# Linear attention and a gated feed-forward block in one planned stream: the last group's results in a room of their own, and the whole order planned anew

## The chip, the cores and the metric

One Trainium2 chip, one core of it. The metric is the device time of one execution in microseconds (us). A core has five engines that run beside each other, each in its own fixed order: TensorE (PE in the profile, its weight loads PEld), VectorE (DVE), ScalarE (ACT), GpSimd (POOL) and SyncE (SP). Any of SP, ACT and POOL can issue a DMA; the core's 16 DMA engines carry all of them out.

## What is computed

For 8 batches of 8 heads with 576 positions and 64 features per head, a linear attention with position weights, and on its output, as 4608 tokens of 512 features, a gated feed-forward block:

```python
r = np.maximum(x, 0.0)                                   # x is q or k
phi = np.concatenate([r * cos_w, r * sin_w], axis=-1)    # weights by position
kv  = np.einsum('bhsf,bhsd->bhfd', k_p, v)              # per head: (2*64) x 64
z   = np.sum(k_p, axis=2)
out = q_p @ kv / (q_p @ z + 1e-6)
...
g = x @ w_gate;  val = x @ w_val                         # 512 -> 1536
y = (g * sigmoid(g) * val) @ w_out                       # 1536 -> 512
```

(The last lines of each part are written shorter here.) Inputs and result are float32; inside, products take 16-bit operands and sum in float32.

## The kernel before

**Batches.** Each batch's q, k and v come by DMA on POOL into 16-bit tiles. ScalarE takes the relu of k, VectorE multiplies v by the two position weights, and 72 small matmuls (`kv_job`, L715) give kv and z. For batches from 2 on, the relu of q and its second, tangent-weighted half are written into the tile `r_q` (`feature_jobs`), which one DMA transposition on SP turns into `phit` (L838). Batches 0 and 1 go another way: TensorE turns their queries (`turned_tile`, L1296), one tile of 128 tokens in a burst of 8 transpositions, for tiles 4 to 8; a relu and a multiplication by tangents follow.

**Tiles.** A tile is 128 tokens (`tile_jobs`): 8 or more matmuls (L778, L784) into two banks of PSUM, ScalarE's denominator `den` (L796), VectorE's reciprocal `rec` (L802) and the multiplication into one of four slots `x` (L806). SP then turns x into `xT` by a DMA transposition (`turn_job`, L746); tiles 4 to 7 are turned by TensorE instead (L754). Two tiles at a time may hold their banks.

**Groups.** Four tiles make a group of 512 tokens; there are nine, 0 to 8. Gate and value products are done with seven block products instead of eight (`block_jobs`, L976; M1 to M7, with sums on VectorE and a ScalarE copy of M1 into the bank that M6 adds to), some value products plainly (`plain_val`, L1051). ScalarE takes silu (L1035), VectorE multiplies (L1060, L1071) into `ht`. The output product (`out_jobs`, L1141) is done with seven products P1 to P7 again; its four quarters are evicted into a room of the buffer `ob`: e11 (from P2), ev and then e22 (P7, P5), e21 (P4) and e12 (P3). VectorE's sums L1184 and L1198 join the products. A pair of tiles shares a room of 128 x 2 x 512 float32; there are two rooms. POOL stores groups 1 to 7 (L1110), SP group 0. In the last group P6, P5 and P3 are cut in halves, and `store_two_jobs` (L1236) stores each quarter as soon as it is written, on SP and ACT.

**The order.** Nothing in the loop order decides what runs when. Every operation is a `Job` with a duration per engine, the jobs it follows, the rooms it takes and gives back (banks, slots, `ob` rooms), and at build time `order_once` plans them all on the five engines: TensorE by rank, the others by due time, both shaken by a seed that changes every 10 us (`SEEDS`). A room is free again when the last job that gives it back is `done`, for a DMA some time after its planned end (`dma`, `tail`, `LATER`). Then each engine's instructions are emitted in the planned order, and the chip keeps that order; real waits are by semaphores. So what the plan puts ahead of an instruction on its engine runs ahead of it, whenever the chip is ready.

Of the kernel before, what the change touches and what calls it, by code (L numbers as in the profile page):

```python
# [11 lines left out]
FP32 = mybir.dt.float32  # L12
BF16 = mybir.dt.bfloat16
FP16 = mybir.dt.float16
AF = mybir.ActivationFunctionType
ALU = mybir.AluOpType
# [3 lines left out]
def kernel(  # L20
# [10 lines left out]
    nc = tc.nc  # L31
    B, H, S, D = q.shape
    P = 128
    G = H // 2
    J = G // 2
    SH = 64
    NC = S // SH
    d_model, d_ff = moe_w_gate.shape
# [14 lines left out]

    consts = ctx.enter_context(tc.tile_pool(name="consts", bufs=1))
    rawq = ctx.enter_context(tc.tile_pool(name="rawq", bufs=3))
    rel = ctx.enter_context(tc.tile_pool(name="rel", bufs=1))
    xtp = ctx.enter_context(tc.tile_pool(name="xtp", bufs=3))
    psum = ctx.enter_context(tc.tile_pool(name="psum", bufs=1, space=bass.MemoryType.PSUM))

# [27 lines left out]
    NSG, NM7, NX = 9, 3, 4  # L87
# [10 lines left out]
    late = phi_all.rearrange("p a b -> p (a b)")[:, LATE:LATE + 8 * J * D1 + 16 * J * SH]  # L98
    assert LATE >= NPHI and late.shape[1] + LATE <= 2 * NPHI
    ob_all = consts.tile([P, 2, 2, d_model], FP32, name="ob")  # L100
    raw_kv = consts.tile([P, 2, 2, G, NC, D], BF16, name="raw_kv")
    free_sg = list(range(NSG))
    raws = {}
# [62 lines left out]
    ident = consts.tile([P, P], BF16)  # L166
# [5 lines left out]
    late = late[:, 8 * J * D1:].rearrange("p (n e j c s) -> p n e j c s", n=4, e=2, j=J, c=2)  # L172
# [10 lines left out]
    def idle_products(n, cols=P):  # L183
# [34 lines left out]
        out=tab.rearrange("p c e d -> p (c e) d"),  # L218
        in_=csk.rearrange("p c e -> p (c e)").to_broadcast([P, NC * 2, D]),
# [5 lines left out]
    tanT = consts.tile([P, NC + 1, SH], FP16, name="tanT")  # L225
# [25 lines left out]
    for j in range(2):  # L251
        t = (phi_all.rearrange("p a b -> p (a b)")[:, 0:V2_1].rearrange(
            "p (g c e w) -> p g c e w", g=G, c=NC, e=2) if j else
            consts.tile([P, G, NC, 2, W], BF16, name=f"v2_{j}"))
# [21 lines left out]
    st = {}  # L276
# [234 lines left out]
    for word in words:  # L511
        word, _, eng = word.partition("@")
        op, a, b = re.match(r"([A-Za-z]+)(\d+)\.?(\d*)", word).groups()
        whole, a, part = b not in ("0", "1") or a != "0", int(a), int(b or 0)
# [39 lines left out]
        else:  # L554
            tiles = [int(x) for x in b]
# [25 lines left out]
    jobs = []  # L581
# [6 lines left out]
    def d2(n):  # L588
        return 70 + n / 1.92 + PAD
# [13 lines left out]
    def sc(n, sbuf=False):  # L603
        return 69 + n / 1.2 + (27 if sbuf else 0) + PAD

    def pe(occ, fn, key, **kw):
        return Job({"PE": occ}, fn, key=key, **kw)
# [7 lines left out]
    def bank(r):  # L615
        if r.n == 1:
            return banks[:, r.at[0]]
        lo, hi = sorted(r.at)
        return banks[:, lo:hi + 1:hi - lo]
# [15 lines left out]
    def relu_on(eng, out, in_):  # L635
        relu_op("act" if eng == "ACT" else "dve", out, in_)

    J_ = {("kv", 0): []}
    KV1_AT = 11.9
    TAN_AT = 9.0  # L640
    T8_AT = 15.5
    HALF_AT = (12.2, 12.6, 13.2, 13.8)
# [21 lines left out]
    tt = nc.vector.tensor_tensor  # L664
# [186 lines left out]
    def feature_jobs(b):  # L851

        loaded_q = [J_["load", b, "q"]] if b > 3 else []
        landed = 0.0 if loaded_q else LOADED["q", b]
        phis = []
        before = J_.get(("turned", b - 1), [])

        def home():
            if (b, "q") not in st:
                st[b, "q"] = rel.tile([P, G, NC, 2, D], BF16, name="r_q")  # L860
            return st[b, "q"]
        if b in PHI_ACT:
            for c in range(NC):
                for w in range(2):
                    def fn(j, c=c, w=w):
                        nc.scalar.activation(out=home()[:, :, c, w], in_=raws[b, "q"][:, :, c], func=AF.Relu,
                                             scale=tanq[:, c:c + 1] if w else 1.0)
                    phis.append(Job({"ACT": 412}, fn, after=loaded_q + before + J_["tanq"], rel=landed))
        else:
            for g in range(0, G, 2):  # L870
                def fn(j, g=g):
                    relu_on(j.eng, home()[:, g:g + 2, :, 0], raws[b, "q"][:, g:g + 2])
                phis.append(Job({"DVE": d4(1152)}, fn, after=loaded_q + before, rel=landed))
            for c in range(NC):
                def fn(j, c=c):
                    nc.scalar.activation(out=home()[:, :, c, 1], in_=raws[b, "q"][:, :, c], func=AF.Relu,  # L876
                                         scale=tanq[:, c:c + 1])
                phis.append(Job({"ACT": 430}, fn, after=loaded_q + before + J_["tanq"], rel=landed))
            J_["q_read", b] = list(phis)
        J_["phi", b] = phis  # L880
        return phis
# [232 lines left out]
    obs = {}  # L1114

    def ob_of(t):
        return ob_all[:, obs[t // 2].at[0], t % 2]

    def pair_of(p):
        return ob_all[:, obs[p].at[0]]  # L1120

    def out_jobs(tg, key):
        last = tg == NTG - 1
        t0 = tg * OUT
        ts = token_sum_jobs(tg)
        rooms = {0: Room("ob"), 1: Room("ob")}
        for p in range(2):
            obs[t0 // 2 + p] = rooms[p]

# [101 lines left out]
    def store_two_jobs(t, cols, after, queues):  # L1231
        for e in range(2):
            def fn(j, e=e):
                (b, c), (b1, _) = divmod(2 * t + e, NC), divmod(2 * t + 2 + e, NC)
                assert b == b1
                {"SP": nc.sync, "ACT": nc.scalar}[j.eng].dma_start(  # L1236
                    out=out_v[b, c:c + 3:2, :, cols].rearrange("c p f -> p c f"),
                    in_=pair_of(t // 2)[e * SH:(e + 1) * SH, :, cols])
            Job({queues[e]: 560}, fn, after=after, tail=3000.0)

    def plain_out_jobs(key):
        rooms = [Room("ob"), Room("ob")]
# [33 lines left out]
    for lo, hi in ((0, 2), (2, 4)):  # L1276
        def fn(j, lo=lo, hi=hi):
            o = raws[1, "k"][:, lo:hi]
            relu_on(j.eng, o, o)
# [2 lines left out]
    kv_job(1, (0, KV1_AT / 16), rk + vm)  # L1282
    plain_out_jobs((0, 0.76, 0.015))

    def turned_tile(t, key):

        r = Room("bank")
        slots = [(0, NC - 1), (1, 0)] if t == 4 else [(1, 2 * t - 9), (1, 2 * t - 8)]
        mine = late[:, 2 * (t % 2):2 * (t % 2) + 2]

        def fn(j):
            ps = bank(r).bitcast(BF16).rearrange("p (y e s) -> p y e s", e=2, s=SH)
            for jj in range(J):
                for n, (b, c) in enumerate(slots):
                    for i in range(2):
                        nc.tensor.transpose(out=ps[i * D:(i + 1) * D, 2 * jj + n].rearrange("p e s -> p (e s)"),  # L1296
                                            in_=raws[b, "q"][:, 2 * jj + i, c], identity=ident)
        mm = pe(240, fn, key, after=[], get=[r], rel=LOADED["sa" if t < 6 else "sb", 1])
        for b, c in slots:
            J_.setdefault(("q_read", b), []).append(mm)  # L1300
        old = J_["tile_mm"][-2:-1] if t > 5 else []

        def fn(j):
            relu_on(j.eng, mine[:, 0].rearrange("p e j c s -> p e (j c) s"),
                    bank(r).bitcast(BF16).rearrange("p (y e s) -> p e y s", e=2, s=SH)[:, :, 0:2 * J])
        re_ = Job({"ACT": sc(512), "DVE": 352}, fn, after=[mm] + old, put=[r])
        c0 = NC - 1 if t == 4 else 2 * t - 9

        def fn(j):
            tt(out=mine[:, 1].rearrange("p e j c s -> p (e j) (c s)"), in0=mine[:, 0].rearrange("p e j c s -> p (e j) (c s)"),  # L1310
               in1=tanT[:, c0:c0 + 2].rearrange("p c s -> p (c s)").unsqueeze(1).to_broadcast([P, 2 * J, P]), op=ALU.mult)
        J_["turned tile", t] = [re_, Job({"DVE": d2(512)}, fn, after=[re_])]

    J_["tile_mm"] = []
    for t in range(4, 9):
        turned_tile(t, (0, (HALF_AT[t - 4] - 0.6) / 16) if t < 8 else (0, T8_AT / 16))
        tile_jobs(t, (0, HALF_AT[t - 4] / 16) if t < 8 else (1, 1.0), t < 8)
        J_["tile_mm"].append(J_["tiles", 1][-1])
    J_["kvd_free"] = J_["tile_mm"][0:1]

    def fn_t(n):
# [71 lines left out]
    for tg in range(1, NTG):  # L1393
        b = tg + 2
# [40 lines left out]
    TILES_AT_ONCE = 2  # L1435
    DMA_MARGIN = 0.0
    EARLY = 9000.0
    SIZE = {"sg": NSG, "m7": NM7, "x": NX, "ob": 2, "tile": TILES_AT_ONCE}
    AHEAD = 18000.0
    SLACK = 1600.0  # L1440
    LOOSE = 8000.0
# [11 lines left out]
    def order_once(nominal, seeds):  # L1453
# [8 lines left out]
        while ready:  # L1462
            j = ready.pop()
# [79 lines left out]
        while n_left:  # L1543
# [43 lines left out]
            j.done = t + j.engs[e] + (TAIL[e] if j.tail is None else j.tail)  # L1587
            if j.dma:
                moved[0] = max(t + j.dma[0], moved[0]) + j.dma[1]
                j.done = moved[0] + LATER  # L1590
            at[e] = t + j.engs[e]
            n_left -= 1
            for r in j.get:
# [14 lines left out]
            for s, _ in succ[j]:  # L1608
                missing[s] -= 1
                if not missing[s]:  # L1610
                    learn(s)
        return max(j.done for j in jobs if "PE" in j.engs)

    RESERVE = 1
    LATER = 2200.0
    SEEDS = (9809, 17028, 79282, 23851, 85677, 79440, 78841, 69575, 80126, 93490, 42418, 59393, 0, 20917, 95217, 13415, 85644, 62013, 51029, 24021, 0, 84984, 14392, 87705, 77482, 88068, 0, 0)
    SHAKE = 1500.0
    WINDOW = 10000.0
    PACK = True
# [40 lines left out]
```

## Time and profile before

| | |
|---|---|
| median of three runs | 301.06 us (301.02 to 301.19) |
| the profiled execution | 300.46 us, span 298.7 us, granted TensorE clock 0.998 |
| busy TensorE, VectorE, ScalarE, POOL | 291.3, 250.9, 199.5, 70.6 us |
| transposition of a tile on SP (xT<-x, 28 times) | median 4.5 us from issue to landing |
| last group's stores (L1236, 8 times) | 2.4 to 3.0 us from issue to landing |

The span runs from the first instruction to the last; the profiled execution's own time is 1.8 us longer. The page lists busy time by engine, the chain of work that ended last (followed back from the last instruction through whatever released each step), and groups of instructions; queries of the trace list waits, timelines of a stretch, and one tile's or line's instructions. In a timeline line stand the start in us, the time, the engine, the line in the kernel, the operation and its tiles, and in brackets the idle time before it and what ended it. "ACTq" and "SPq" are DMA issues. A matmul's record is longer than its place in the stream: matmuls of 256 columns start every 109 ns.

### The profile page before, as it was taken

The numbers are of one execution on the slowest core, as the hardware profiler recorded it, in microseconds if no ns is written. First come the engines' busy times: TensorE is split into PE (matmuls) and PEld (weight loads), VectorE is DVE, ScalarE is ACT, GpSimd is POOL, SyncE is SP. The second block draws the span as 40 slices with busy tenths as digits, with TensorE's granted clock in tenths as the row PEclk, the third lists the DMA queues.
The fourth block names the chain that finished last, engine by engine and source line by source line (L and its number), as shares of the span: only waits on it lengthen the run. The fifth ranks groups of instructions, "written<-read, shape, count | busy, mean of one in ns | idle before, by whom it ended". The sixth has DMA issues, their size and how long they took to land.

```text
span 298.7 us, 8071 instructions
## 1 busy us (share of the span) xinstructions
PE 291.3 (98%) x3244; PEld 238.4 (80%) x3244; DVE 250.9 (84%) x513; ACT 199.5 (67%) x421; POOL 70.6 (24%) x126
## 2 busy tenths in 40 slices
PE   8999999999999999999999999999999999999992
PEld 4697465676777888888988888888888898888882
DVE  7878996978977898989979997988879868976972
ACT  6664346979558986797699588996475556645520
POOL 7954620030042130221233203200220050002020
PEclk9999999999999999999999999999999999999999
DMA  7999999999989999269899892770370074002025
GB/s 259 228 196 198 202 206 208 201 217 204 193 137 172 157 213 160 72 126 189 131 177 234 143 155 69 145 160 2 73 142 2 0 131 83 2 2 70 2 70 142
DMA packets 71781, 40.89 MB, mean 137 GB/s; under 512 B 48704, under 2 KB 68672, under 8 KB 71744
## 3 DMA queue, kind: packets, MB, share of 16 engines
q0 software_dynamic: 24992, 24.91, 49.8%
q1 hardware_dynamic: 46320, 15.08, 27.1%
q8 instruction: 25, 0.41, 0.6%
q10 hardware_dynamic: 432, 0.39, 0.4%
q14 instruction: 12, 0.10, 0.1%
HBM read 37.75 MB, written 9.44 MB: 158 GB/s over the span
## 4 chain that ended last, share of the span: by engine, by line
PE 88%; DVE 5%; DMA 4%; ACT 1%; issue 1%; ACTq 0%; DVEq 0%
PE banks L976 43%; PE banks L1141 23%; PE banks L1250 4%; PE banks L437 4%; PE banks L903 4%; DMA xT<-x 3%; PE banks L715 2%; PE banks L784 2%; PE banks L1051 2%; DMA wo_sb<-in_v_dram 1%; DVE ht L1060 1%; DVE sums L1092 1%; DVE v L292 1%; PE banks L778 1%; PE banks L371 1%; ACT sg L1035 1%
## 5 line engine op out<-in xcount | busy, mean ns | idle before, releaser
L1110 POOL DMA_DIRECT2D out_dram<-ob x56 | 29.4, 533 | 148.6 <-ACT ob L629 104.7
L1035 ACT ACTIVATE sg<-banks 128x512 bf16<-128x512 f32 x72 | 41.3, 596 | 9.9 <-PE banks L976 9.5
L627 ACT COPY banks<-banks 128x512 f32<-128x512 f32 (+1 forms) x53 | 30.2, 577 | 17.8 <-PE banks L1141 6.0
L1071 DVE TENSOR_TENSOR ht<-sg,banks 128x512 f16<-128x512 bf16 x60 | 40.3, 680 | 1.7 <-PE banks L976 1.6
L976 PEld LDWEIGHTS <-wg_sb 128*128 128x128 f16 x384 | 36.9, 98 | 5.5 <-issue 0.4
L1141 PEld LDWEIGHTS <-ht 128*128 128x128 f16 x384 | 37.0, 98 | 4.9 <-issue 0.3
L976 PEld LDWEIGHTS <-wgs_sb 128*128 128x128 f16 x368 | 35.6, 98 | 5.5
L996 DVE TENSOR_TENSOR banks<-m,banks 128x512 f32<-128x512 f32 x44 | 30.3, 691 | 7.0 <-ACT m L627 4.3
L629 ACT ACTIVATE ob<-banks 128x512 f32<-128x512 f32 x34 | 19.9, 595 | 22.7 <-PE banks L1141 22.3
L976 PEld LDWEIGHTS <-wv_sb 128*128 128x128 f16 x320 | 31.2, 98 | 3.9 <-DVE x L806 0.2
L976 PE MATMUL banks<-kvt,wgs_sb 128*128 128x256 f16 x236 | 33.6, 273 | 0.0
L1141 PEld LDWEIGHTS <-sums 128*128 128x128 f16 x288 | 27.9, 98 | 3.6 <-DVE sums L1092 0.2
L627 ACT COPY m<-banks 128x512 f32<-128x512 f32 x44 | 25.6, 589 | 6.5 <-PE banks L976 6.4
L976 PE MATMUL banks<-xT,wg_sb 128*128 128x256 f16 x192 | 28.5, 273 | 0.3 <-ACT banks L627 0.3
L1141 PE MATMUL banks<-wo_sb,ht 128*128 128x256 f16 x192 | 25.9, 273 | 0.0
L1141 PE MATMUL banks<-wt_sb,sums 128*128 128x256 f16 x192 | 24.3, 273 | 0.0
L976 PE MATMUL banks<-xT,wv_sb 128*128 128x256 f16 x160 | 23.9, 273 | 0.0
L806 DVE TENSOR_TENSOR x<-banks,rec 128x512 f16<-128x512 f32 x32 | 21.7, 687 | 2.0 <-DMA xT<-x 0.3
L976 PE MATMUL banks<-kvt,wg_sb 128*128 128x256 f16 x168 | 23.1, 273 | 0.0
L1141 PE MATMUL banks<-wt_sb,ht 128*128 128x256 f16 x192 | 22.8, 273 | 0.2 <-DVE banks L1184 0.2
L876 ACT ACTIVATE r_q<-raw_q,tanq 128x256 bf16<-128x256 bf16 x45 | 20.1, 503 | 0.0
L1035 ACT ACTIVATE sg<-m 128x512 bf16<-128x512 f32 x24 | 15.1, 629 | 7.1 <-DVE m L1004 7.0
(157 smaller groups left out, 542.4 us busy)
## 6 DMA issues: line engine op xcount, KB each, us to landing
out_dram<-ob POOLq DMA_DIRECT2D x56, 128.0 KB, 3.4
raw_kv<-in_k_dram POOLq DMA_DIRECT2D x7, 576.0 KB, 6.9
raw_q<-in_q_dram POOLq DMA_DIRECT2D x12, 288.0 KB, 9.6
raw_kv<-in_v_dram POOLq DMA_DIRECT2D x6, 576.0 KB, 8.9
out_dram<-ob SPq DMA_DIRECT2D x13, 128.0 KB, 2.5
wg_sb<-in_moe_w_gate_dram POOLq DMA_DIRECT2D x5, 256.0 KB, 8.8
wv_sb<-in_moe_w_val_dram POOLq DMA_DIRECT2D x5, 256.0 KB, 9.4
wo_sb<-in_v_dram SPq DMA_DIRECT2D x2, 576.0 KB, 4.1
```

The costliest lines, as they stand in the source:

```text
L437: nc.tensor.matmul(out=st["f", tg, fc, lo][i], lhsT=(wg_sb, wv_sb)[i][:, kc, fs], rhs=xT[tg][:, ts, kc], start=(kc == 0), stop=(kc == KC - 1))
L627: nc.scalar.copy(out=out, in_=in_)
L629: nc.scalar.mul(out=out, in_=in_, mul=mul)
L806: tt(out=one(x_all, x).rearrange("p (y e d) -> p e y d", e=2, d=D), in0=view()[:, :, :, 0:D], in1=rec_all[:, t % 4].rearrange("p (e y) o - ...
L876: nc.scalar.activation(out=home()[:, :, c, 1], in_=raws[b, "q"][:, :, c], func=AF.Relu, scale=tanq[:, c:c + 1])
L903: nc.tensor.matmul(out=bank(r), lhsT=w[:, kc, fc * P:(fc + 1) * P], rhs=xT[tg][:, :, kc], start=(kc == 0), stop=(kc == KC - 1))
L976: nc.tensor.matmul(out=to[:, i], lhsT=a[:, c, 2 * u + i], rhs=x()[:, :, c], start=first and i == 0 and c == 0, stop=c == KH - 1, skip_grou ...
L996: tt(out=bank(c), in0=one(m7_all, m).rearrange("p i x -> p (i x)"), in1=bank(b), op=ALU.add)
L1035: nc.scalar.activation(out=gates(rooms[w])[:, :, jh * HT:(jh + 1) * HT], in_=src, func=AF.Silu, scale=DOWN)
L1071: tt(out=ht[:, 4 * u + w:4 * u + w + 3:2, jh * HT:(jh + 1) * HT], in0=gates(rooms[w])[:, :, jh * HT:(jh + 1) * HT], in1=src.rearrange("p ( ...
L1110: {"POOL": nc.gpsimd, "SP": nc.sync, "ACT": nc.scalar}[j.eng].dma_start(out=out_v[idx // NC, idx % NC][:, cols], in_=ob_of(t)[e * SH:(e + ...
L1141: nc.tensor.matmul(out=to, lhsT=a[:, kc, i * P:(i + 1) * P], rhs=b[:, kc], start=first and kc == 0 and i == 0, stop=kc == HC - 1, skip_gro ...
```

## The change

Three things. The last group's two rooms are no longer those of `ob`: they lie in the memory of `r_q`, which becomes a constant tile (kind "last ob" in the plan). The queries of tiles 4 and 5, and of 6 and 7, are turned in one burst of 16 transpositions into one bank; tile 8 stays alone. And the plan is made anew: the last group's stores have other durations in it, the plan's end is that of the last job of all and not of the last TensorE job, and the seeds are others. So the order of nearly every engine past the first 32 us differs, with the same work. Line numbers behind the head grow by one.

```diff
-    rel = ctx.enter_context(tc.tile_pool(name="rel", bufs=1))
...
+    rq_all = consts.tile([P, G * NC * 2 * D], BF16, name="r_q")
+    ob_last = rq_all[:, 0:8 * d_model].bitcast(FP32).rearrange("p (a b f) -> p a b f", a=2, b=2)
...
-                st[b, "q"] = rel.tile([P, G, NC, 2, D], BF16, name="r_q")
+                st[b, "q"] = rq_all.rearrange("p (g c w d) -> p g c w d", g=G, c=NC, w=2)
...
-        return ob_all[:, obs[p].at[0]]
+        return (ob_last if obs[p].kind == "last ob" else ob_all)[:, obs[p].at[0]]
...
-        rooms = {0: Room("ob"), 1: Room("ob")}
+        rooms = {n: Room("last ob" if last else "ob") for n in range(2)}
...
-            Job({queues[e]: 560}, fn, after=after, tail=3000.0)
+            Job({queues[e]: 660}, fn, after=after, tail=1300.0, dma=(700.0, 560.0))
...
-    def turned_tile(t, key):
+    def turned_tiles(ts, key):
...
+            for m, t in enumerate(ts):
+                for jj in range(J):
+                    for n, (b, c) in enumerate(slots[t]):
+                        for i in range(2):
+                            nc.tensor.transpose(out=turned(m)[i * D:(i + 1) * D, 2 * jj + n].rearrange("p e s -> p (e s)"),
+                                                in_=raws[b, "q"][:, 2 * jj + i, c], identity=ident)
+        mm = pe(200 + 236 * len(ts), fn, key, after=[], get=[r], rel=LOADED["sa" if ts[-1] < 6 else "sb", 1])
...
-    for t in range(4, 9):
-        turned_tile(t, (0, (HALF_AT[t - 4] - 0.6) / 16) if t < 8 else (0, T8_AT / 16))
-        tile_jobs(t, (0, HALF_AT[t - 4] / 16) if t < 8 else (1, 1.0), t < 8)
-        J_["tile_mm"].append(J_["tiles", 1][-1])
+    for ts in ((4, 5), (6, 7), (8,)):
+        turned_tiles(ts, (0, (HALF_AT[ts[0] - 4] - 0.6) / 16) if ts[0] < 8 else (0, T8_AT / 16))
+        for t in ts:
+            tile_jobs(t, (0, HALF_AT[t - 4] / 16) if t < 8 else (1, 1.0), t < 8)
+            J_["tile_mm"].append(J_["tiles", 1][-1])
...
-    SIZE = {"sg": NSG, "m7": NM7, "x": NX, "ob": 2, "tile": TILES_AT_ONCE}
+    SIZE = {"sg": NSG, "m7": NM7, "x": NX, "ob": 2, "last ob": 2, "tile": TILES_AT_ONCE}
...
-                j.done = moved[0] + LATER
+                j.done = moved[0] + (j.tail if j.tail < LATER else LATER)
...
-        return max(j.done for j in jobs if "PE" in j.engs)
+        return max(j.done for j in jobs)
...
-    SEEDS = (9809, 17028, 79282, 23851, 85677, ...)
+    SEEDS = (0, 62553, 49105, 61770, 0, ...)
```

## The prediction

> **What bounds the kernel now.** I read the page first, then the chain of work that ended last, then the waits of TensorE, and then the timelines of the stretches that these pointed to.
>
> ```profile
> PE 291.3 (98%) x3244; PEld 238.4 (80%) x3244; DVE 250.9 (84%) x513; ACT 199.5 (67%) x421; POOL 70.6 (24%) x126
> ...
> PE 88%; DVE 5%; DMA 4%; ACT 1%; issue 1%; ACTq 0%; DVEq 0%
> ```
>
> TensorE bounds it: it is busy nearly everywhere and carries 88% of the chain. The granted clock is 0.998, so nothing is to be had there. Only three things can move the time: TensorE's own work, the places where it waits, and the end behind its last matmul. The waits of TensorE and of its weight loads (us in total, times, longest) are few:
>
> ```profile
> PE banks L976 <- ACT banks L627: 0.3, 1, 0.3
> PE banks L1141 <- DVE banks L1184: 0.2, 1, 0.2
> ...
> PEld L784 <- DVE x L806: 0.6, 2, 0.3
> PEld L1051 <- DVE x L806: 0.6, 1, 0.6
> ```
>
> A busy matmul covers part of a wait, so I measured each by the starts of consecutive matmuls against their usual distance (109 ns for 256 columns, 216 ns for 512). Past 32 us that gives 0.24 at 73.5 (L1051), 0.34 at 82 (L1141), 0.43 at 87 (L976), 0.20 at 128.3 and 0.20 at 129.2 (L784), 0.12 at 217 and 0.05 at 187: 1.6 us in all. The end, from the chain, and ScalarE's timeline there:
>
> ```profile
> 284.63 8.09 PE banks L1141 x74
> 292.75 0.43 DVE ob L633
> 293.18 0.35 ACTq L1236
> ...
> 293.74 0.60 ACT ob L629
> ```
>
> ```profile
> 292.81 0.72 ACTq L1236 DMA_DIRECT2D out_dram<-ob  x1
> 293.74 0.60 ACT L629 ACTIVATE ob<-banks 128x512 f32<-128x512 f32 x1 [5.41 <-PE banks L1141]
> 293.90 1.66 ACTq L1236 DMA_DIRECT2D out_dram<-ob  x2
> ```
>
> The copy at 293.74 is e11, the quarter whose product P2 was complete four microseconds earlier. It stands behind a store issue in ScalarE's order, since its room was group 7's. The last SP and ACT stores, issued at 294.54 and 294.93, are e11's, and the span ends at 298.7.
>
> **The end: last group's own room.** It adds no instruction. In the new emitted order ScalarE's copies ev and e11 both stand before its first store issue and wait for TensorE alone; e11's stores go out first, on SP and on ACT. What is late next is e12: the last matmul ends at 293.37, the VectorE copy of its second half runs 293.40 to 293.83, and its two stores can be issued at 293.86 (SP) and about 293.9 (ACT). So the last issue comes 1.0 us earlier (294.93 - 293.9). Issue to landing at L1236 is 2.4 to 3.0 us, median 2.8, before and after; the last landing then moves by 0.9 to 1.05 with ACT's own rows (2.8 to 3.0), by up to 1.5 with the shortest. I take **-1.0**. The VectorE waits for group 7's stores that vanish took about 0.05 us each beside the 0.69 us copy of e21, so they are worth nothing. The own room reuses r_q, whose last reader (the transposition of batch 7, 7.5 us from its issue at 193.0) is long done; cost nothing.
> In the new tail P6a, P6b and P5a follow each other without P2b between. P5a needs VectorE's sum of P6a: 0.31 us from a last matmul's start to a VectorE start (293.09 to 293.40), 0.43 for the sum, 0.06 back, 0.80, against 7 x 0.109 = 0.76: **+0.05**.
> The Trainium skill ("DMA: Bandwidth & Descriptors", "Anatomy of one DMA") gives a DMA some 2.0 us fixed plus its bytes over 436 GB/s. For 128 KB that would be an estimate of 2.3 us and a last landing 0.5 us sooner than mine. The rows 2.4 to 3.0 disagree upwards, and they decide.
>
> **Turned queries.** Forty transposes before, forty after. Tiles 4 and 5 already stood together; tiles 6 and 7 did not. The chain has x16 at 0.57 us and x8 at 0.34, so joining one pair saves 2 x 0.34 - 0.57 = **0.1**. Both relus then read one bank; tile 7's first use is two microseconds off in either order, so nothing waits.
>
> **The order anew**, counted from the emitted orders. TensorE's instructions are the same 3244. Visits to the 16-bit batch-side products (L715, L778, L784, L1296) between the others cost about 0.09 us at their entry; there are 36 before and 34 after: **-0.2**.
> Waits that go. At 87, M6 followed M1 after 0.87 us of other matmuls, while the ScalarE copy between them takes 0.58 plus two handovers and stood behind another; now a whole kv product (1.2 us) stands between: -0.43. At 128 and 129 four tiles stood within 3 us, with two tile rooms; now the third comes 2.6 us or more behind the first, and tile to x takes 2.0 to 2.3: -0.4. Together **-0.85**.
> A wait that grows. VectorE idles for tile 10's x in this stretch, and SP shows why:
>
> ```profile
> 72.13 0.64 DVE L1060 TENSOR_TENSOR ht<-sg,banks 128x512 f16<-128x512 bf16 x1
> 73.03 0.69 DVE L806 TENSOR_TENSOR x<-banks,rec 128x512 f16<-128x512 f32 x1 [0.26 <-DMA xT<-x]
> ```
>
> ```profile
> 53.45 7.57 SPq L838 DMA_TRANSPOSE phit<-r_q  x1
> 61.13 3.08 SPq L1110 DMA_DIRECT2D out_dram<-ob  x5
> 64.31 1.28 SPq L746 DMA_TRANSPOSE xT<-x  x1
> 65.63 0.62 SPq L1110 DMA_DIRECT2D out_dram<-ob  x1
> ```
>
> Tile 10 takes the x slot of tile 8, whose transposition (8.6 us, in the chain 64.31 to 72.90) must have read it. In the new order all eight group-0 stores stand between batch 2's transposition and tile 8's; before, two went ahead and one behind, so three more now, at 3.08 / 5 and a gap, 0.64 us each. Against that, the two stores that no longer precede it leave 256 KB less traffic beside the slow 7.57 us transposition (others of its kind issue in 4.6), so I put its end 1.0 sooner. Tile 8's issue: 60.0 + 0.1 + 8 x 0.64 = 65.2; between 64.3 (all 1.9 regained) and 66.5 (nothing, and features 0.3 later). Plus 8.6: landing 73.8, bounds 72.9 and 75.1. Without that wait x could start at 73.4, for tile 11's reciprocal, whose input ScalarE ends at 73.05, now stands ahead of it. So x starts at about 73.9 and TensorE's tenth value product (L1051), which takes x's bank, at 73.9 + 0.69 + 0.06 = 74.65; TensorE gets there at 73.64 (73.54 now, with 0.1 us more matmuls ahead of it in the new order): 1.0 instead of 0.24. From x to the sum L1184 VectorE has 8.4 us of work (before 8.5), and P5 behind it waits 0.2 instead of 0.34. Sum 1.2 against 0.58: **+0.65**, bounds 0 and 1.8. Nothing gives this back: VectorE is full until 88, TensorE afterwards.
> The Trainium skill ("DMA: Bandwidth & Descriptors", "Issuing engines are not separate DMA queues") says that transfers of all issuers run on the same 16 engines and interleave. This speaks against the new order: eight stores and 1.7 MB of loads (k, v and q) share them with this one transposition. The trace agrees, 8.6 us against a median of 4.5 for its kind. By that rule alone, with no traffic taken away, the upper bound above would hold.
> Other new waits: every stage is ordered anew; five waits of 0.05 to 0.43 came with the old order outside this stretch, 1.0 in all, so between 0 and 1.0; I take **+0.3**, since the new order has fewer tiles close together. One eviction-side job moves from VectorE to ScalarE (a 0.4 us relu): nothing.
>
> **Sum:** -1.0 + 0.05 - 0.1 - 0.2 - 0.85 + 0.65 + 0.3 = -1.15. The profiled execution took 300.46 (span 298.7 and 1.8 around it); so 299.3 there. The median of the three runs is 301.06, 0.6 higher, so **299.9**.
>
> **Rivals.**
> A, the gain is eaten at 73 us: tile 8's transposition lands at 75.1 or so, TensorE waits 2.3 + 0.2 there, +1.9 instead of +0.65. Then 301.1, no change that can be seen (0.2%, 0.6 us, is about what a measurement tells). For it: the 8.6 us row and the three stores. Against: less traffic before it.
> B, slower: the loads of batch 3 and batch 4's queries, which wait only for batch 2's transposition, go out earlier, and the transposition of tile 8 ends only with them, at about 76.5 as they ended before. x then starts at 76.6, TensorE loses 3.9 there, +3.3: 302.6. It decides when that landing passes 75.6, where the loss reaches 2.4 and the whole +0.6. Against: before, its packets moved beside the loads, at a quarter of the engines' time.
> C, the own room does nothing: SP, with five store issues, ends as late as before. Then -0.15, 300.9. Against: SP's e12 issue at 293.86 follows its previous one, ending at 293.41, with room to spare.
> The Trainium skill ("DMA: Bandwidth & Descriptors", "Queues, rings and completion order") has each engine take turns between queues, packet by packet. By that rule B would have no chance; the rows of one such transposition do not exclude it.
>
> **Chances.** Forecast 0.62 (its own range 299.0 to 300.4), A 0.23, C 0.05, B 0.10. Faster 0.62, same 0.28 (A and C), slower 0.10. The range, 298.9 to 301.4, takes in A and C and leaves out B and some low tail.
>
> **What would show it.** Right: e11's copy before ScalarE's first store issue, and about 4.3 us from the last matmul's end (293.37) to the span's end (298.67) instead of 5.3; no wait at 87 and 128; VectorE's x of tile 10 at 73.9, behind its DMA. Wrong: x of tile 10 past 75, or a wait of TensorE of over 0.5 us anywhere behind 90, or the span's end still 5 us behind the last matmul.

## The result and the profile after

The changed kernel takes 305.55 us in the median of four runs (304.43 to 306.71); the kernel before took 301.04 beside it. The ratio is 1.0152, with a 95% interval of 1.0105 to 1.0199: **slower by 4.5 us**, where 1.2 us faster was forecast and 301.4 was the upper end of the range. The profiled execution took 306.71 us with a span of 304.9, against 300.46 and 298.7. A second series of the same kernel gave 306.1 (run e5 below).

The page of the changed kernel, busy time and then the chain of work that ended last:

```profile
PE 294.3 (97%) x3244; PEld 239.2 (78%) x3244; DVE 250.8 (82%) x512; ACT 199.3 (65%) x422; POOL 70.0 (23%) x126
...
PE 36%; DMA 3%; DVE 2%; issue 0%; ACT 0%; DVEq 0%
```

The work is the same, yet TensorE is busy 3.0 us longer with the same 3244 matmuls (1.0 of it in the head, the first 32 us, which the change leaves alone), and the rest of the span's growth is idle time. The chain covers only 41% of the span: it goes back to a load at 176.53 and breaks off there, so it does not show where most of the time was lost. The waits of TensorE do (us in total, times, longest):

```profile
PE banks L1052 <- DVE x L807: 2.9, 1, 2.9
PE banks L977 <- DMA xT<-x: 1.2, 1, 1.2
PE banks L187 <- DVE zeros L182: 1.0, 1, 1.0
PE banks L785 <- DVE x L807: 0.9, 3, 0.3
```

The third of these stands in the head. Of the waits of before, those at 87 (L976 behind a ScalarE copy) and at 128 and 129 are gone, as forecast. In their place stands one of 2.9 us at the plain value product that waits for VectorE's x. VectorE's timeline there, and SP's:

```profile
73.10 0.44 DVE L803 RECIPROCAL rec<-den 128x8 f32<-128x8 f32 x2
76.42 1.29 DVE L807 TENSOR_TENSOR x<-banks,rec 128x512 f16<-128x512 f32 x2 [2.88 <-DMA xT<-x]
```

```profile
53.68 6.39 SPq L839 DMA_TRANSPOSE phit<-r_q  x1
60.12 5.33 SPq L1111 DMA_DIRECT2D out_dram<-ob  x8
65.55 14.71 SPq L747 DMA_TRANSPOSE xT<-x  x4
```

Tile 10's x starts at 76.42, not at 73.03 as before nor at 73.9 as forecast: it takes the slot of tile 8, whose transposition, issued at 65.55 behind all eight stores of group 0, landed at 76.3. TensorE, by the starts of its matmuls, stands still for 3.06 us from 74.1. Then comes a second loss. TensorE's timeline, and the same stretch in windows of 5 us (busy times and counts of PE, PEld, DVE, ACT and POOL, then the granted clock, the DMA share and GB/s; the last line is the kernel before):

```profile
73.25 1.03 PE L1052 MATMUL banks<-xT,wv_sb 128*128 128x512 f16 x4
77.17 4.45 PE L1052 MATMUL banks<-xT,wv_sb 128*128 128x512 f16 x12 [2.90 <-DVE x L807]
```

```profile
70.00:75.00 5.00, 4.27 (x40) 2.58 (x38) 3.50 (x9) 5.00 (x14) 0.00 (x0) 1.00 1.27 185
75.00:80.00 5.00, 2.83 (x8) 1.12 (x9) 3.08 (x5) 2.48 (x5) 0.00 (x0) 0.76 0.85 139
80.00:85.00 5.00, 4.99 (x42) 3.61 (x41) 4.37 (x9) 1.12 (x3) 0.00 (x0) 0.90 0.90 171
...
75.00:80.00 5.00, 5.00 (x41) 3.71 (x39) 5.00 (x10) 2.27 (x5) 0.00 (x0) 1.00 1.32 153
```

Twelve matmuls of 512 columns take from 77.17 to 81.46, 4.29 us instead of 12 x 0.216 = 2.59. Eight of them start 427 ns apart, twice the usual distance, and the granted clock of those windows is 0.76 and 0.90 where before it was 1.00: in the trace it stands at 0.50 for 3.4 us, from 77.6 to 81.0, and at 1.00 on both sides. That is 1.7 us more, and with the head's 1.0 it is most of what TensorE's busy time grew by.

**Where the 6.2 us of the profiled span went:** wait at 74: 3.06 instead of 0.24, +2.8; slow clock behind it, +1.7; waits behind 90: 1.27 at 173.6 (a transposition of a tile), 1.23 in three at 186 to 190 (x), 0.41 at 250.5 and 0.26 in small ones, 3.2 instead of 0.6, +2.6; waits at 82 and 87, -0.6; the end, -0.9; bursts and visits, some -0.2; and the head, code that the change leaves alone, +0.6 (TensorE's L693 at 32.77, L692 before at 32.18). Sum 6.0.

The end came as forecast. ScalarE's timeline there:

```profile
293.90 0.59 ACT L630 ACTIVATE r_q<-banks 128x512 f32<-128x512 f32 x1
295.15 0.60 ACT L630 ACTIVATE r_q<-banks 128x512 f32<-128x512 f32 x1 [0.66 <-PE banks L1142]
295.78 5.80 ACTq L1237 DMA_DIRECT2D out_dram<-r_q  x3
```

Both copies now stand ahead of the first store issue. From the last matmul's end (300.45) to the span's end (304.90) are 4.45 us, before 5.31.

### The profile page after: what moved, and what is told of

It reads as the page before. It is cut to its first block, busy times and chain, and to the rows that moved or that the text cites. A ratio compares the mean times of both kernels' runs of the same rounds, so it can differ in the third digit from the quotient of the medians.

```text
span 304.9 us, 8061 instructions
## 1 busy us (share of the span) xinstructions
PE 294.3 (97%) x3244; PEld 239.2 (78%) x3244; DVE 250.8 (82%) x512; ACT 199.3 (65%) x422; POOL 70.0 (23%) x126
## 5 line engine op out<-in xcount | busy, mean ns | idle before, releaser
L630 ACT ACTIVATE ob<-banks 128x512 f32<-128x512 f32 x32 | 18.9, 596 | 21.7 <-PE banks L1142 21.6
L293 DVE TENSOR_TENSOR v<-raw_kv,tab 128x1152 bf16<-128x1152 bf16 x27 | 19.5, 748 | 1.4 <-DMA raw_kv<-in_v_dram 1.4
```

Of the source, the lines that this page charges most:

```text
L293: nc.vector.tensor_tensor(out=v2s[b == 1][:, g, :, :, 0:D], in0=(first if b == 0 and g == 0 else {"v": raw_of(b, "v")})["v"][:, g].unsquee ...
L630: nc.scalar.mul(out=out, in_=in_, mul=mul)
```

## The experiments

**Theory:** tile 8's transposition came late because loads and stores hold up its queue; the late x idled TensorE, and the idle time lowered the clock. **Rivals:** the loss stands in the other waits of the new order; the transposition is slow wherever it is issued; the slow matmuls have a cause of their own; it takes the whole new order to make the loss. The table shows all runs, each beside the kernel before on the same chip. The wait is that of TensorE at 73 to 74, from the starts of its matmuls.

| run | median us | ratio to before (95%) | wait at 74 | slow matmuls |
|---|---|---|---|---|
| changed | 305.55 | 1.0152 (1.0105 to 1.0199) | 3.06 | yes |
| e1 room alone, old order | 300.4 | 0.9984 (0.9975 to 0.9993) | 0.49 | no |
| e2 changed, own slot for tile 10 | 299.75 | 0.9964 (0.9936 to 0.9992) | 0 | no |
| e3 changed, transposition forward | 300.2 | 0.9970 (0.9960 to 0.9981) | 0.08 | no |
| e4 changed, two loads held | 300.47 | 0.9992 (0.9970 to 1.0014) | 0.09 | no |
| e5 changed, again | 306.1 | 1.0164 (1.0141 to 1.0186) | 3.06 | yes |
| e6 old order, stores ahead | 305.06 | 1.0144 (1.0118 to 1.0170) | 3.60 | yes |
| e7 e3 and a long wait made | 306.34 | 1.0186 (1.0162 to 1.0209) | 4.05 | yes |
| e8 e3 and a shorter one | 302.47 | 1.0053 (1.0033 to 1.0073) | 2.21 | yes |
| e10 old order, transposition forward | 300.64 | 0.9985 (0.9973 to 0.9997) | 0 | no |
| e11 e10 and the room | 299.65 | 0.9954 (0.9940 to 0.9969) | 0 | no |
| e9 changed, e2 and e3 together | 299.85 | 0.9958 (0.9941 to 0.9975) | 0 | no |
| e12 e9, tiles 21 and 23 forward | 300.77 | 0.9994 (0.9983 to 1.0005) | 0 | no |
| e13 e9 again | 300.09 | 0.9973 (0.9962 to 0.9983) | 0 | no |
| e14 e11 again | 299.81 | 0.9964 (0.9950 to 0.9977) | 0 | no |

### Is it the wait for tile 8's slot? (e2)

```diff
-    x_all = consts.tile([P, NX, d_model], FP16, name="x")
+    x_all = consts.tile([P, NX + 1, d_model], FP16, name="x")
...
+        J_["x room", t] = x
...
-    best = (end,)
+    best = (end,); J_["x room", 10].at = [NX]
```

> The changed kernel with a fifth x slot that tile 10 alone uses, so that it no longer waits for the transposition of tile 8; nothing else moves. Theory: that wait (3.06 us of TensorE at 73.9) and the fall of the granted clock right behind it (nine matmuls 0.21 us longer each, 1.9 in all) are one loss; x of tile 10 starts at about 73.5, no slice shows a low clock, and the time falls by 4.3 to 4.9, to about 301.0. Rival one: the slow matmuls have another cause than the idle time before them; then they stay and the time falls by 2.9 only, to 302.6. Rival two: the loss stands in the other waits of the new order (173 to 250 us); then it falls by under 1.

One address differs; every instruction keeps its place, and tile 8's transposition is as late as in the changed kernel (it lands at 75.9). VectorE's x of tile 10, here with that of tile 11, no longer waits:

```profile
72.67 0.44 DVE L804 RECIPROCAL rec<-den 128x8 f32<-128x8 f32 x2
73.02 1.25 DVE L808 TENSOR_TENSOR x<-banks,rec 128x512 f16<-128x512 f32 x2
```

No matmul is slow, and the median falls by 5.8, to 299.75. The theory holds and both rivals fall. The time is even 1.2 better than expected; in this execution the waits at 173 and beyond are smaller too (1.1 instead of 2.5).

### Why did it land late? (e3, e4, e6)

e3 moves one SP instruction, e4 lets GpSimd wait between the load of k and that of v:

```diff
-    best = (end,)
+    best = (end,); J_["xT", 8].start = 34317.0      # e3
...
+        load_k3(j)                                  # e4
+        nc.gpsimd.tensor_copy(out=hold2, in_=xT[2][0:1, 0, 0, 0:2])
```

> The changed kernel with one SP instruction moved: the transposition of tile 8 goes out right behind that of batch 2 (at about 60.1 instead of 65.55), ahead of the eight stores of group 0, which go out 1.3 later. Theory (the transposition stands in the queue behind stores that the loads of batch 3 hold up): it lands before the loads begin to move or soon after, between 64.7 and 68.7, x of tile 10 waits for nothing, and the time falls by 4.3 to 4.9, to about 301.0. Rival: the place on SP does not matter, since it is the loads that slow the transposition itself; it lands past 73 and the time falls by under 1.5.

> The changed kernel with the loads of v for batch 3 and of q for batch 4 held on GpSimd until the transposition of tile 8 has landed (one tiny copy more); the load of k stays where it is, and so do the stores and the transposition on SP. Theory (the loads hold up the stores and the transposition): with a third of their bytes left beside it, the transposition issued at 65.55 lands at 71 to 73, TensorE waits 0.3 or less at 74, and the time falls by 4 to 4.9. Rival: it is the three more stores ahead of it, and the later issue, that make it late; it lands past 75 still and the time stays within 1 of the changed kernel.

SP and then VectorE in e3:

```profile
60.53 1.25 SPq L747 DMA_TRANSPOSE xT<-x  x1
61.88 5.40 SPq L1111 DMA_DIRECT2D out_dram<-ob  x8
```

```profile
73.38 0.44 DVE L803 RECIPROCAL rec<-den 128x8 f32<-128x8 f32 x2
73.73 1.28 DVE L807 TENSOR_TENSOR x<-banks,rec 128x512 f16<-128x512 f32 x2
```

Both remedies work, 5.4 and 5.1 us under the changed kernel, a little more than expected; e4's ten runs lie far apart (299.85 to 302.74). In e3 the transposition lands at 63.0, 2.5 us behind its issue, so it is not slow wherever it is issued; in e4 it lands at 72.6. So neither the place on SP nor the loads alone make it late: it takes the two together, and the rivals of both runs fall. How they act shows in the DMA packets that began in each microsecond, counted from the traces (loads are 1152-byte packets on POOL's queue; stores, of 2048, and transpositions, of 256, are on SP's queue; 512 of the last kind are one tile's, and the last 23 counted for the changed kernel are tile 9's):

```
us      changed: loads stores transp.   e4: loads stores transp.
63             0     92       0            0    110       0
64            21     62       0           14     32       0
65            91      0       0           58     36       0
66           166      0       0          125     28       0
67           116      5       0          141      2       0
68           114     42       0          116     25       0
69            89     77       0           54    117       0
70           108     60      29            4     40     478
71           114      7     102            0      8      25
72            79      1      71            0      0       9
73           141      0     151            0      0     512
74           132      0     140           21      0       0
75           158      0      42           91      0       0
```

In the changed kernel SP's queue moves next to nothing from 65 to 68, while the first load of batch 3 (512 packets) goes out, although its last three stores (192 packets) are issued by 65.5 and the transposition right behind them. The stores go first, until 71, and the 512 packets of tile 8 then go out from 70.3 to 75.8, some one beside each packet of the loads. In e4, once the load of k is out and the others are held, 478 of the same 512 go in one microsecond, and tile 9's 512 all in the one at 73. In the kernel before, the queue stood still as well, from 66 to nearly 68, but the transposition was next in it: the stores ahead of it were through.

e6 makes only this exchange in the kernel before: all eight stores between the two transpositions, nothing else.

```diff
...
+    for n, j in enumerate(stores[:2]):
+        j.start = J_["turned", 2][0].start + 1.0 + n
+    J_["xT", 8].start = stores[-1].start + 1.0
```

> The kernel before (its order, its shared room) with one thing of the change: on SP, all eight stores of group 0 stand between the transposition of batch 2 and that of tile 8 (before: two ahead of it, five between, one behind). Theory: this alone makes the loss. The transposition of tile 8 is issued at about 65.3, lands at 75.5 to 76.5, x of tile 10 starts at about 76.3, TensorE waits about 3 at 73.5, the matmuls behind it are slow for up to 2 more, and the time is 304 to 306. Rival: the new order around it is needed too (tile 11's reciprocal ahead, VectorE fuller, the matmuls earlier); then it lands at 74 or less and the time stays within 1.5 of the kernel before.

Its VectorE and its clock at that place:

```profile
76.27 0.69 DVE L806 TENSOR_TENSOR x<-banks,rec 128x512 f16<-128x512 f32 x1 [3.61 <-DMA xT<-x]
```

```profile
75.00:80.00 5.00, 2.98 (x8) 1.06 (x9) 3.14 (x6) 0.09 (x1) 0.00 (x0) 0.60 0.84 148
```

305.06, 4.1 over the kernel before. The order of three stores and the two transpositions on SP is enough to make the loss; the rest of the change is not needed for it. It acts in two ways that no run parts: three stores more are ahead of tile 8's transposition, and batch 2's transposition, with two stores fewer ahead, lands sooner and lets the loads go sooner (k's at 62.6, in the changed kernel 62.7, before 63.9), as rival B said, so that they catch these stores in the queue.

### Does the idle time lower the clock? (e7, e8, e5)

In e3, which has no wait at 74, spare VectorE products ahead of tile 10's x make one, with no DMA late:

```diff
+        for _ in range(9):              # e8: 5
+            tt(out=spare, in0=wv_sb[:, 0, 0:d_model], in1=wv_sb[:, 1, 0:d_model], op=ALU.mult)
+        mul10(j)
```

> The kernel with the transposition of tile 8 put forward (which had no wait at 74), and nine spare VectorE products of 128x512 (some 3 us in all, results unused) right ahead of x of tile 10, so that TensorE waits there as long as in the changed kernel, with no transposition late. Theory: an idle TensorE lowers the granted clock. Then about nine matmuls take 427 ns instead of 216 behind the wait, and the time rises by the wait and 1 to 2 more: 4 to 5. Rival: the slow matmuls came from the late transposition and the loads beside it; then none is slow here and the time rises by the wait alone, about 3.

> The same with five of the spare products, so that TensorE waits about 1.6 there. If the clock falls only behind an idle time near three microseconds, no matmul is slow and the time rises by 1.6; if any such idle time lowers it, some are slow and the rise is 2 to 3.5.

A spare product took 0.42 us, and one started every 0.46, instead of the 0.33 reckoned with, so the waits were 4.05 and 2.21. TensorE behind them, in e7 and then in e8:

```profile
78.02 5.30 PE L1053 MATMUL banks<-xT,wv_sb 128*128 128x512 f16 x12 [3.89 <-DVE x L807]
```

```profile
75.56 4.45 PE L1053 MATMUL banks<-xT,wv_sb 128*128 128x512 f16 x12 [2.05 <-DVE x L807]
```

By starts, the twelve take 5.09 (78.02 to 83.11) and 4.29 us (75.56 to 79.85) instead of 2.59. The clock falls with the idle time, whatever caused it, and 2.2 us can be enough; the theory holds, and e8's guess of a limit near three does not. Waits of 1.3 us or less lowered it in none of these executions. In the traces the low clock is 0.50 and lasts 3.41 us in the changed kernel, e5 and e8, and twice that, 6.83, in e6 and e7, where it fell before the wait was over (in e7 at 76.9). The Trainium skill ("TensorE: Matmul & The Clock Gate", "Part 1: The HAM clock gate") says that a monitor halves the clock after an idle window of about 3.4 us, that the window runs freely, and that the clock comes back after a busy one. The half rate (427 against 216 ns) agrees, and so do the slow stretches of one and two times 3.41 us; the 2.2 us of idle time do not agree with a full idle window.

> The changed kernel once more, as it is, on the same chip as the next three, to see which of its waits belong to it and where its runs differ (304.4 to 306.7). Theory: tile 8's transposition lands at 75.5 to 76.5 each time, TensorE waits 2.5 to 3.3 at 74 and slow matmuls follow, so 304 to 307 again; the runs differ in how long the clock stays low. The waits at 173.6 (1.27) and 186 to 190 (1.2) were absent with the same order when tile 8's transposition came earlier; if they come back here, they hang on this shift, if not, they are chance. Rival: the profiled execution was an odd one, and this one shows no such wait and about 300.

306.1, with the same 3.06 and slow matmuls in the profiled execution: the theory holds. The waits at 168 to 190 came back as well, 2.3 us in all; but they do not hang on the late x alone, since e2 and e9, without it, have 1.1 and 1.3. Of its four runs two have a mean granted clock of 1.000 (305.39 and 305.52) and two of 0.991 and 0.992 (306.68 and 306.71): the clock does not fall in every execution, and 1.2 us hang on it. In e8 it is the same, 1.000 with 301.92 and 302.16, 0.994 with 302.77 and 303.34. That explains part of the 2.3 us between the changed kernel's runs, not all: its first series had 304.43 at 0.990.

### What are the room and the new order worth? (e1, e10, e11, e9)

> The kernel before with the last group's own room alone; the order of every other instruction is the one of before, only the copy e11 and its two stores come forward. If the room is worth what the prediction gave it, the span ends about 4.3 us behind the last matmul instead of 5.3 and the time is 0.9 to 1.0 under the kernel before (300.0 to 300.2). Rival: the room does nothing, since the last stores land no sooner; then within 0.2 of the kernel before (301.0).

> The kernel before, with its order and its shared room, and only the transposition of tile 8 put ahead of the stores of group 0 that still stood before it on SP (five of eight). Theory: the wait of 0.24 at 73.5 goes, and nothing else is in it: 0.1 to 0.3 under the kernel before. Rival: the place matters more than the trace shows, 0.5 or more under it.

> The same, with the last group's own room beside it. By the prediction the room takes 0.9 to 1.0 off; by the run with the room alone 0.5. So 299.8 to 300.3; against the run without the room the difference prices the room a second time.

e1 is only 0.5 faster, between its theory (0.9 to 1.0) and its rival (0.2), though its span ends 4.57 us behind the last matmul; in this execution tile 10's x cost 0.49, and the head was 0.5 later. With that wait removed on both sides, e11 against e10 gives the room alone: 299.65 against 300.64, **-1.0**, and 4.58 against 5.47 us behind the last matmul. So by medians the room is worth 0.5 in one comparison and 1.0 in the other, by the traces 0.7 and 0.9. e10 took off 0.5, where 0.1 to 0.3 was expected and 0.5 was its rival's; its interval, 0.1 to 0.8, does not decide between them.

> The changed kernel (new order, turned bursts, own room) with both remedies: a fifth x slot for tile 10 and the transposition of tile 8 ahead of the stores. If the small terms of the prediction are real (bursts -0.1, visits -0.2, waits that go -0.85, other new waits +0.3: -0.85 in all), it is 0.5 to 0.9 under the old order with both remedies, at 299.1 to 299.7. Rival: the new order is worth nothing in itself; then it is within 0.25 of that kernel.

299.85, level with e11: the rival holds, and no gain of the new order with its bursts can be seen. The trace shows the gains (of the old order's 1.2 us at 82, 87, 128 and 129 only 0.17 is left, at 79) and what eats them: 0.54 at 168.6, 0.48 at 182.6 and 0.25 at 183.4.

### What eats the new order's gains? (e12, e13, e14)

In the new order two things meet at 160 to 190. SP issues batch 6's transposition ahead of tiles 21 and 23, and VectorE has batch 7's v products ahead of tile 24's x. VectorE in the changed kernel:

```profile
184.33 0.76 DVE L293 TENSOR_TENSOR v<-raw_kv,tab 128x1152 bf16<-128x1152 bf16 x1 [1.38 <-DMA raw_kv<-in_v_dram]
185.00 0.20 DVE L803 RECIPROCAL rec<-den 128x8 f32<-128x8 f32 x1
185.12 0.71 DVE L293 TENSOR_TENSOR v<-raw_kv,tab 128x1152 bf16<-128x1152 bf16 x1
185.74 0.68 DVE L807 TENSOR_TENSOR x<-banks,rec 128x512 f16<-128x512 f32 x1
```

The x of tile 24 stands behind a product that waits for the load of v, and that load goes out only when batch 6's transposition has landed. e12 turns the first of the two around in e9:

```diff
+    J_["turned", 6][0].start = J_["xT", 23].start + 1.0
```

> The changed kernel with both remedies, and on SP the transpositions of tiles 21 and 23 ahead of that of batch 6 (in the new order they stand behind its eight microseconds of issue; in the old one all four tiles go first). Theory: TensorE's wait for a transposition at 168 to 174 (0.5 to 1.3, in some executions none) and what follows at 182 to 190 come from this; then they are gone or under 0.3, the time is 0.3 to 0.8 under the same kernel without the exchange, and its runs lie closer together (under 1 from lowest to highest). Rival: batch 6's own transposition, now some 4 later, is what TensorE needs next; then the wait at 182 grows and nothing is won.

> The changed kernel with both remedies once more, for comparison on the same chip: 299.3 to 300.3 in the median, spread over 2 or more, with waits at 168 to 184 of 0.7 or more in all.

> The old order with the own room and tile 8's transposition forward once more, on the same chip: 299.5 to 299.9, spread under 0.6, no wait of over 0.45 behind 90.

In the profiled execution of e12 the wait at 168 is gone, but VectorE now idles 1.90 for the load of v:

```profile
178.68 0.76 DVE L293 TENSOR_TENSOR v<-raw_kv,tab 128x1152 bf16<-128x1152 bf16 x1 [1.90 <-DMA raw_kv<-in_v_dram]
```

TensorE waits 1.0 at 179.8 and 0.74 behind it, and the median is 300.77 against 300.09: the rival holds, one lateness was changed for another, and e12's runs lie no closer together (300.11 to 301.52). e13's median came within its range, but its profiled execution has none of the waits at 168 to 184, and its runs spread over 1.4, not 2. That execution took 299.56, as long as e14's (299.57) with all the waits of the old order; its head was 0.7 later. e14 came within its range, but spread over 1.0 instead of under 0.6. Both latenesses hang on batch 6's transposition. From its issue on SP to GpSimd's copy that waits for its landing, the executions of the new order show, with the sum of the waits at 168 to 190 beside it:

| | e13 | e4 | e3 | e8 | e7 | e9 | e2 | changed | e5 |
|---|---|---|---|---|---|---|---|---|---|
| issue to landing, us | 13.6 | 13.6 | 13.9 | 14.2 | 14.5 | 14.7 | 15.4 | 15.7 | 16.6 |
| waits at 168 to 190, us | 0 | 0 | 0 | 0.4 | 0.7 | 1.3 | 1.1 | 2.5 | 2.3 |

Up to 13.9 nothing waits; each microsecond more costs roughly one. By these nine executions the new order's waits there go with how fast this one transposition runs; no run changes that time alone. That they also spread the runs is not shown: e9 has 298.87 to 301.76 and e11 299.57 to 299.84, but the old order has 299.85 to 301.33 in e10. Why the transposition takes 13.6 us in one execution and 16.6 in another stays open.

e11 (299.65, and 299.81 in e14) beats both kernels: the old order, the own room, and tile 8's transposition five stores earlier.

## Why the prediction was wrong

- **The end, -1.0: right.** -0.9 in the trace, -1.0 between e10 and e11, though only -0.5 in e1. P5a's +0.05 was 0.10 (at 296.15). The estimate that the prediction set beside it, from "Anatomy of one DMA" in the Trainium skill's "DMA: Bandwidth & Descriptors", uses a fit that the page gives for DMAs issued by GpSimd; the last stores are SP's and ACT's, so their rows of 2.4 to 3.0 us do not speak against it.
- **Bursts -0.1, visits -0.2, waits that go -0.85:** the waits at 87, 128 and 129 went as counted. The two small terms could not be told from the noise of the runs.
- **The wait that grows, +0.65 with bounds 0 and 1.8: the step that failed.** It measured +2.8, 3.06 us against 0.24. Its place, its chain and the issue time were right (65.2 forecast, 65.55 measured; batch 2's transposition 1.1 us earlier, as forecast, though of the other five of its kind only three issue in 4.6 us and two take 5.8 and 6.8). "Plus 8.6: landing 73.8" was not: the time from issue to landing was taken over from before as if it belonged to the transposition. It was 10.7 us and the landing 76.3. By the packets, before had 3.3 us of waiting in the queue, 4.8 of transfer beside the loads and 0.5 to the landing; the changed kernel had 4.8, 5.5 and 0.5, since three stores still stood in the queue ahead of the transposition, held up by the same load. In e4, with the loads of v and q held, 478 of the 512 packets took one microsecond. The upper bound of 75.1 held the issue time uncertain, but not this. Rival B had the place right (76.5 forecast, 76.3 measured) and got 0.10, in part by luck: its reason was that the transposition ends only with the loads, and the last of them landed at 78.5. What spoke against it, that the packets "moved beside the loads, at a quarter of the engines' time", was an average over a stretch in which they first did not move at all. The prediction also held against B the Trainium skill's rule ("DMA: Bandwidth & Descriptors", "Queues, rings and completion order") that an engine takes turns between queues packet by packet. From 71 on the trace agrees (151 against 141 packets in the microsecond at 73); from 65 to 68 it shows no such turns, with 373 packets of one queue to 5 of the other. Why the turns begin so late stays open.
- **A term that was missing: the clock.** Even B's price, 302.6, left out that a long wait of TensorE can cost more than its length: 1.7 us of slow matmuls behind 3.06 us of idle time. The prediction read the clock of before (0.998) as "nothing is to be had there" and did not ask what an idle TensorE would do to it. With both, B's case would have stood near 304.
- **Other new waits, +0.3 with bounds 0 and 1.0: mis-sized.** 3.2 us behind 90 in the profiled execution, and 0.3 to 2.9 in the others of this order. The old order's total was taken as a measure of any order's; but the new one had put x behind a load and tiles behind a long transposition, and both were there to be counted in the emitted order. Two of the signs of being wrong that the prediction named came: x of tile 10 past 75, and waits of over 0.5 us behind 90.

## What to carry to other kernels

The time from issue to landing of a DMA is no property of it: before carrying it into a new order, split it by its packets into the wait in the queue and the transfer, and count what stands ahead in its queue and which loads are let go beside it. A wait of TensorE of 2.2 us or more cost more than its length here in 16 of 20 executions (by their mean clocks), since the matmuls behind it ran at half speed; waits of 1.3 us or less did not in any profiled one. An order that wins small waits by putting engines' work close behind DMAs gave them back here in the executions in which the DMA was slow.

## What the runs showed of the hardware

- The granted clock fell behind idle times of 2.2, 3.06, 3.6 and 4.05 us, but not in every execution; the clock was then 0.50 for 3.41 or 6.83 us, and matmuls of 512 columns started 427 ns apart.
- SP's queue moved next to nothing (5 packets to 373) for three microseconds while one load of 576 KB on POOL's queue went out; later the two shared about one packet for one (151 to 141 at 73).
- The first microseconds of unchanged code took two forms. The scalar operation at L206 (L205 before) took 0.22 or 0.23 us in before, e3, e6 and e8 to e12, and 0.84 in the changed kernel, e1, e2, e4, e5, e7, e13 and e14, beside GpSimd's fill of 128 x 520 elements. The end of TensorE's head (L692 or L693) moved between 32.0 and 33.2, as much as many of the terms in the sum, but not with these two forms: e10 has the short one and 33.2, e14 the long one and 32.3. The Trainium skill ("SBUF — State Buffer", "Who interferes with whom") tells of a port pair of these two engines that one of them holds for a whole instruction; that both can lose fits it: in before it is GpSimd's fill at L178, beside VectorE's cast, that took 0.81 instead of 0.20. No run here was made to show it.
